# Pairwise merge products in the attention's triangular inverse, an earlier decode of float64 weights, and the experts' low weight parts on another engine

## The chip, the cores and the metric

One core of a Trainium2 chip runs the whole program. The metric is the device time of one execution in microseconds (us); a kernel's time is the median of its runs. A profiled execution of the same program gives the trace from which all rows below come. Engines are named as in the profile: PE (TensorE), PEld (its weight loads), DVE (VectorE), ACT (ScalarE), POOL (GpSimd), SP (SyncE, which here issues nearly all DMAs; SPq is its queue).

## The reference, cut to what matters

Three layers follow one another: a recurrent attention over 768 steps, a routed mixture of eight experts (one expert for each token), and a dense layer with a leaky activation. The matrices `w_in` and `w_out` of the last layer arrive as float64.

```python
# attention: B, H, S, D = 4, 8, 768, 40, all float32
for t in range(S):
    y[:, :, t] = np.einsum('bhd,bhde->bhe', rt, state)
    Sa = np.einsum('bhde,bhe->bhd', state, at)
    state_decay = state * wt[:, :, None, :] - np.einsum('bhd,bhe->bhde', Sa, bt)
    state = state_decay + np.einsum('bhd,bhe->bhde', vt, kt)
x = attn_out.transpose(0, 2, 1, 3).reshape(B * S, H * D)        # 3072 x 320
# experts: w1 (8, 320, 1024), w2 (8, 1024, 320), float32
logits = x @ w_gate; expert_idx = np.argmax(logits, axis=1)
for e in range(8):
    xe = x[expert_idx == e]
    out[expert_idx == e] = gate_w * (np.maximum(xe @ w1[e], 0) @ w2[e])
# last layer: w_in (320, 2048), w_out (2048, 320)
h = out @ w_in
y = (np.maximum(h, 0) + alpha * np.minimum(h, 0)) @ w_out
```

## The kernel before, in words

**Attention** (class `Attention`). The 768 steps are cut into chunks of 64. Four chunks of two batches (16 heads) are a group; there are six groups. Inside a chunk the recurrence becomes products with T, the inverse of a unit triangular 64x64 matrix per head and chunk. `inverse` finds T in two steps. On DVE a loop of 31 steps inverts all 32x32 diagonal blocks at once (`tmp`, `ut`). Then `diagonal` copies the blocks into the tiles `tt`, one tile for each half of a group, and two rounds of small products on PE fill the off-diagonal 32x32 block: `zp` = l1 times the high diagonal block, a copy to `z` on ACT, `yp` = t11 times z, and a copy with a minus sign into `tt` on ACT. A `tt` tile holds for each of two chunks (c2) and eight head pairs (u) a 128x128 block with two heads (q) on its diagonal. These rounds are called merges here: 6 groups x 2 halves x 2 products = 24 products, of 32 matmuls each before the change. `tt` is a ring of three tiles. The main loop has 48 slots; the plan in `run` lays the preparation of the next groups between them. `Router.tiles` turns finished outputs into token rows `xr` and scatters them to `xs_d` in DRAM by GpSimd's indirect DMA.

**Experts** (class `Moe`). For expert e the rows of `xs_d` are loaded (`xe`), transposed and split into a high and a low part; the hidden layer is made in eight blocks f of 128 columns. For each f PE makes `ph` (two PSUM buffers, so PE can be one block ahead), ACT makes `hh` = relu(ph), DVE makes what is missing of it (`hh` for the last 64 columns, and the low part `hl`), and PE then adds the block to the sums `po`. The first expert does its first 256 tokens on their own (`ehh`, `ehl`) and the other 192 after them, in the same eight blocks. At the end `ye` is taken from the sums and written to DRAM.

Beside this, `prep_expert(e + 1, ...)` loads the next expert's weights in six pieces into a ring of three `raw` tiles, ACT makes their high parts and one engine subtracts these from `raw` to give the low parts (`we`, L1058, L1060, L1073). And `decode` turns the 20 pieces of the float64 matrices into float32: DMA of 512 KB into `r64` (two buffers), three integer operations on DVE (`dec`, L214, L215, L216 in `f64_bits`), a range test on ACT (`sq`), DMA back to DRAM.

**The order of the work.** Only the first group's start is written out by hand for DVE, POOL and ACT. All else is placed by a scheduler at build time, which fixes one order for each engine and for SP's queue; at run time each engine goes through its list and waits where an operand is missing. The last layer (`run` from L1237 on) works on 6 blocks of 512 tokens and is the same in both kernels.

Of the kernel before, what the change touches and what calls it, by code (L numbers as in the profile page):

```python
# [8 lines left out]
F32 = mybir.dt.float32  # L9
# [10 lines left out]
P = 128  # L20
# [268 lines left out]
class Attention:  # L289
# [9 lines left out]
    def __init__(self, tc, ctx, k, wP, kbP, aP, rvP, vrow, rt):  # L299
# [34 lines left out]
        self.d1s = ring("d1s", 1, [PP, nw], V, (every, 1e-10), (lambda t: t.rearrange("p (c t) -> p c t", t=CW)[:, :, C:], 1.0), dt=BF16, pool=self.pa)[0]  # L334
        self.d1q = ring("d1q", 1, [PP, nw], V, (every, 0.0), pool=self.pa)[0]
# [21 lines left out]
    def fill(self, out, n):  # L357

        flat = out.rearrange("p c u t -> p (c u t)")
        for _ in range(n):  # L360
            mm(self.nc, flat[:, :P], self.k.ones, self.k.ones, True, True)
# [163 lines left out]
    def inverse(self, o):  # L525
# [8 lines left out]
        for j in range(31):  # L534
            n, m = 31 - j, j + 1
            if o.start:
                tmp = self.pa.tile([P, 256], F32, name="tmp", bufs=1)
                col = ul[:, j, j + 1:]
            else:
                if j == 0:  # L540
                    bank = self.work("tmp", [P, 512], "mg")
                    tmp = bank[:, :256]
                if j in (0, 8, 16):
                    j0, j1 = j, (8, 16, 32)[j // 8]
                    part = bank[:, 256:256 + (j1 - j0) * (32 - j0)].rearrange("p (a b) -> p a b", b=32 - j0)
# [14 lines left out]

        ttc = self.t4("ttc")
# [6 lines left out]
        lows = [slice(q * 64, q * 64 + 32) for q in range(2)]  # L568
        highs = [slice(q * 64 + 32, q * 64 + 64) for q in range(2)]
        both = [(c2, u, q) for c2 in range(2) for u in range(8) for q in range(2)]  # L570
        for half in range(2):
            if half:
                diagonal(1)
# [4 lines left out]
            zp = self.work("zp", [P, 2, 8, 32], "mg" if o.start or half == 0 else "w1")  # L578
            if o.start:
                self.fill(zp, 8)  # L580
            for c2, u, q in both:
                nc.tensor.matmul(zp[lows[q], c2, u], lhsT=l1[highs[q], 2 * half + c2, u, :], rhs=tt[highs[q], c2, u, highs[q]], start=True, stop=True)
            z = self.pa.tile([P, 2, 8, 32], F32, name="z1", tag="z1", bufs=1)
            for lo in lows:
                nc.scalar.copy(z[lo], zp[lo])
            yp = self.work("yp", [P, 2, 8, 32], "mg" if o.start or half == 0 else "w1")
            if o.start:
                self.fill(yp, 8)
            for c2, u, q in both:
                nc.tensor.matmul(yp[lows[q], c2, u], lhsT=t11[lows[q], 2 * half + c2, u, :], rhs=z[lows[q], c2, u, :], start=True, stop=True)  # L590
            for lo, hi in zip(lows, highs):
                nc.scalar.activation(tt[lo, :, :, hi], yp[lo], AF.Copy, scale=-1.0)
# [286 lines left out]
class Router:  # L879
# [39 lines left out]
    def tiles(self, sp, work, b0, t, yt):  # L919

        nc, k = self.nc, self.k
        xr = [sp.tile([P, DM], F32, name="xr", bufs=3) for _ in range(2)]
# [74 lines left out]
class Moe:  # L997
# [142 lines left out]
    def run(self, ctx, to_flag):  # L1140
# [16 lines left out]
        for e in range(E):  # L1157
# [27 lines left out]
            def between(f):  # L1185
# [16 lines left out]
                if (e, f) == (1, 0):  # L1202
# [160 lines left out]
```

## Time and profile before

| | |
|---|---|
| median of 3 runs | 1097.79 us (1097.37 to 1098.29) |
| the profiled execution's own time | 1104.12 us |
| its span, first to last instruction | 1102.4 us |
| PE busy | 995.8 us, 90% of the span |
| DVE busy | 668.2 us, 61% |
| POOL busy | 578.0 us, 52% |
| ACT busy | 531.7 us, 48% |
| mean granted clock of PE | 0.953 |

Busy shares are means over three stages with different limits: attention to about 485 us, experts to about 742 us, the last layer to the end. What a wait costs is read from the stage in which it lies. Matmuls are pipelined, so a row's duration is longer than the step from one matmul to the next.

### The profile page before, as it was taken

To read this page: it belongs to the slowest core of one execution; us is meant where nothing else is said; L and a number is where in the kernel's file an instruction comes from. 1 tells how busy PE (TensorE), PEld (TensorE's weight loads), DVE (VectorE), ACT (ScalarE), POOL (GpSimd) and SP (SyncE) were. 2 spreads that over 40 slices of the span, in tenths; PEclk is the share of its full clock that TensorE was granted. 3 is DMA by queue.
4 is the path that set the end of the run, shared out by engine and by line. 5 is a ranking of instruction groups with operands and counts; after the bars stand their busy time and mean duration, and the time that the engine had idled before them with its cause. 6 is when DMAs were issued, how large, how long until landed. Compare 5 with 4: busy or idle time off the path is not lost.

```text
span 1102.4 us, 25835 instructions
## 1 busy us (share of the span) xinstructions
PE 995.8 (90%) x9981; PEld 883.5 (80%) x9981; DVE 668.2 (61%) x1451; ACT 531.7 (48%) x1255; POOL 578.0 (52%) x592
## 2 busy tenths in 40 slices
PE   3669998889899898889799999999999999999997
PEld 3557777778788777678788889999898898988986
DVE  8895959969688594553679763234444444444532
ACT  3656766677677676644666644431222222221211
POOL 7865665796867544325465544643534343534332
PEclk9669989999899898889999999999999999999999
DMA  4452423333333134417889854420000000000000
GB/s 123 113 188 74 95 66 82 95 87 79 85 84 76 45 71 101 104 37 239 263 278 304 282 162 126 140 70 11 24 25 25 24 25 24 25 24 25 25 1 27
DMA packets 128326, 103.43 MB, mean 94 GB/s; under 512 B 90564, under 2 KB 111044, under 8 KB 128196
## 3 DMA queue, kind: packets, MB, share of 16 engines
q1 hardware_dynamic: 125892, 93.83, 29.8%
q0 software_dynamic: 2304, 7.87, 2.2%
q8 instruction: 81, 1.33, 0.5%
q14 instruction: 49, 0.40, 0.1%
HBM read 79.39 MB, written 22.28 MB: 92 GB/s over the span
## 4 chain that ended last, share of the span: by engine, by line
PE 62%; DVE 21%; DMA 6%; issue 4%; ACT 4%; POOL 3%; SPq 0%; DVEq 0%; POOLq 0%; ACTq 0%
PE ph L243 22%; PE po L243 21%; PE lp L493 3%; PE pp L631 2%; DVE tmp L549 2%; DVE ut L551 2%; DVE s L464 2%; DVE dec L215 2%; DMA raw<-in_moe_w_dram 2%; PE sa L671 2%; PE yc L687 2%; PE rvp L642 2%; DVE va L676 1%; PE ap L517 1%; DVE q L466 1%
## 5 line engine op out<-in xcount | busy, mean ns | idle before, releaser
L234 POOL TENSOR_TENSOR gl<-g,gh 128x512 fp32r<-128x512 f32 x96 | 123.6, 1290 | 214.8 <-ACT gh L233 123.3
L233 ACT ACTIVATE gh<-g 128x512 fp32r<-128x512 f32 x96 | 60.8, 633 | 251.9 <-DVE g L1250 173.2
L1249 DVE TENSOR_SCALAR g<-ph,al 128x512 f32<-128x512 f32 x96 | 72.1, 751 | 160.1 <-POOL gl L234 79.8
L243 PE MATMUL ph<-x2thi,win 128*128 128x512 f32 x480 | 159.5, 397 | 0.0
L243 PE MATMUL po<-wout,gh 128*128 128x320 f32 x768 | 139.0, 310 | 0.0
L243 PEld LDWEIGHTS po<-wout,gh 128*128 128x128 f32 x768 | 122.0, 188 | 5.6
L243 PE MATMUL ph<-x2tlo,win 128*128 128x512 f32 x288 | 114.3, 397 | 0.0
L243 PE MATMUL po<-we,hh 128*128 128x320 f32 x480 | 90.5, 316 | 11.8 <-DVE hh L1122 8.8
L243 PEld LDWEIGHTS ph<-x2thi,win 128*128 128x128 f32 x480 | 88.6, 188 | 14.9
L243 PE MATMUL ph<-xthi,we 128*128 128x448 f32 (+2 forms) x360 | 96.9, 341 | 0.8 <-ACT xthi L273 0.8
L243 PEld LDWEIGHTS po<-we,hh 128*128 128x128 f32 x480 | 73.9, 182 | 16.8 <-DVE hh L1122 10.3
L243 PE MATMUL po<-wout,gl 128*128 128x320 f32 x384 | 82.9, 312 | 0.0
L473 POOL TENSOR_TENSOR abd<-ra,q 40x512 f32<-40x512 f32 x44 | 63.5, 1443 | 25.5 <-PE ap L517 14.0
L493 PE MATMUL lp<-kb,abd 128*128 128x128 f32 x352 | 63.4, 329 | 14.5 <-POOL abd L473 9.6
L243 PE MATMUL ph<-xtlo,we 128*128 128x448 f32 (+2 forms) x216 | 73.4, 341 | 0.3 <-DVE xtlo L276 0.3
L243 PEld LDWEIGHTS ph<-xthi,we 128*128 128x128 f32 x360 | 65.7, 193 | 4.2 <-ACT xthi L273 0.9
L493 PEld LDWEIGHTS lp<-kb,abd 128*128 128x128 f32 x352 | 53.8, 230 | 18.8 <-POOL abd L473 10.2
L1250 DVE SCALAR_TENSOR_TENSOR g<-ph,g 128x512 f32<-128x512 f32 x96 | 66.3, 691 | 3.1
L243 PEld LDWEIGHTS po<-wout,gl 128*128 128x128 f32 x384 | 64.0, 188 | 3.0
L655 POOL TENSOR_SCALAR vg<-sm 40x160 f32<-40x160 f32 x96 | 33.6, 350 | 61.3 <-DVE sm L692 47.7
L551 DVE TENSOR_TENSOR ut<-ut,tmp 128x31 f32<-128x31 f32 (+15 forms) x186 | 62.6, 336 | 3.6
L1058 POOL TENSOR_TENSOR we<-raw,we 128x1024 fp32r<-128x1024 f32 x14 | 34.0, 2441 | 57.3 <-ACT we L1056 56.1
(218 smaller groups left out, 2323.0 us busy)
## 6 DMA issues: line engine op xcount, KB each, us to landing
raw<-in_moe_w_dram SPq DMA_DIRECT2D x16, 512.0 KB
raw<-in_moe_w_dram SPq DMA_DIRECT2D x16, 480.0 KB
kb<-in_kbP_dram SPq DMA_DIRECT2D x44, 160.0 KB
r<-in_moe_w_in_dram SPq DMA_DIRECT2D x10, 512.0 KB
r<-in_moe_w_out_dram SPq DMA_DIRECT2D x10, 512.0 KB
xs_d<-tt SPq DMA_DIRECT2D x8, 560.0 KB
raw<-in_moe_w_dram SPq DMA_DIRECT2D x16, 256.0 KB
wz<-in_wP_dram SPq DMA_DIRECT2D x48, 81.4 KB
```

What stands on the lines that cost most here:

```text
L215: nc.vector.scalar_tensor_tensor(t, up, 0xC0000000, t, op0=ALU.bitwise_and, op1=ALU.bitwise_or)
L233: nc.scalar.activation(hi, src, AF.Copy)
L234: return lo_eng.tensor_tensor(lo, src, f32(hi), op=ALU.subtract)
L243: return nc.tensor.matmul(out, lhsT=lhsT, rhs=rhs, start=start, stop=stop)
L464: nc.vector.tensor_tensor_scan(s[:, ::-1], wz[:, 1:][:, ::-1], self.d1s[:, ::-1], 0.0, ALU.mult, ALU.max)
L473: nc.gpsimd.tensor_tensor(abd[r, :, q * C:(q + 1) * C], ra[r], qc[r, :, :C], op=ALU.mult)
L493: nc.tensor.matmul(lp[:, i], lhsT=abd[:, i, c2, :], rhs=kb[:, i, c2, :], start=True, stop=True)
L551: nc.vector.tensor_tensor(ut[:, j + 1:, :m], ut[:, j + 1:, :m], tv, op=ALU.subtract)
L655: nc.gpsimd.tensor_scalar(self.by2(x.vg[C:PP, :, q, :D]), self.halves(self.sm[q * HQ:q * HQ + D, x.p2]), 1.0, 0.0, op0=ALU.mult, op1=ALU.add)
L1058: eng.tensor_tensor(wt[:, 3 + c, cs], raw, f32(wt[:, c, cs]), op=ALU.subtract)
L1249: nc.vector.tensor_scalar(g, ph, 0.0, al[:, f:f + 1], op0=ALU.min, op1=ALU.mult)
L1250: nc.vector.scalar_tensor_tensor(g, ph, 0.0, g, op0=ALU.max, op1=ALU.add)
```

## The change

Four edits. **Merges:** a product takes both heads of a pair at once: 16 matmuls with 128 contraction rows, 64 columns of weights (the wanted 32 and 32 more whose results are not read) and 64 moving columns. For that the rows of the other head and of the low block must be zero, so `vacant` clears the blocks of `tt` on POOL ahead of each half (not for the first group, whose tiles are cleared as a whole), `z` is one fixed tile that is cleared once at the start, and the copies out of PSUM are four of 256 columns instead of two of 512. **Room:** the first group's `tmp` comes from the ring `t4`, and `xr` has two buffers instead of three. **Low parts:** the experts 1 to 7 get the low parts of their weights from DVE instead of POOL; those of `win` and `wout` stay on POOL. **Decode:** it is called at the first block of expert 0's second part instead of the first block of expert 1.

```diff
+        self.z = ring("z", 1, [P, 2, 8, C], G, (every, 0.0), pool=self.pa)[0]
...
-                tmp = self.pa.tile([P, 256], F32, name="tmp", bufs=1)
+                if j == 0:
+                    tmp = self.pa.tile([P, 1024], F32, name="tmp", tag="t4", bufs=3)
...
+        def vacant(half):
+            if not o.start:
+                for lo, hi in zip(lows, highs):
+                    nc.gpsimd.memset(o.tt[half][lo, :, :, hi], 0.0)
...
+        pairs = [(c2, u) for u in range(8) for c2 in range(2)]
+        out = lambda t, c2, q: t[c2 * 64:c2 * 64 + 32, :, q * 32:q * 32 + 32]
+        heads = lambda t: t.rearrange("p (q s) -> p q s", q=2)
+        wide = lambda t, c, u: t.rearrange("p c u j -> p (c u j)")[:, 32 * (8 * c + u):min(32 * (8 * c + u) + C, 1024)]
...
-            for c2, u, q in both:
-                nc.tensor.matmul(zp[lows[q], c2, u], lhsT=l1[highs[q], 2 * half + c2, u, :], rhs=tt[highs[q], c2, u, highs[q]], start=True, stop=True)
-            z = self.pa.tile([P, 2, 8, 32], F32, name="z1", tag="z1", bufs=1)
-            for lo in lows:
-                nc.scalar.copy(z[lo], zp[lo])
+            for c2, u in pairs:
+                w = wide(l1, 2 * half + c2, u)
+                high = heads(tt[:, c2, u])[:, :, 32:]
+                nc.tensor.matmul(heads(zp[c2 * 64:c2 * 64 + w.shape[1], u]), lhsT=w, rhs=high, start=True, stop=True)
+            z = self.z
+            for c2 in range(2):
+                for q, lo in enumerate(lows):
+                    nc.scalar.copy(z[lo, c2, :, q * 32:q * 32 + 32], out(zp, c2, q))
...
+            for c2, u in pairs:
+                w = wide(t11, 2 * half + c2, u)
+                nc.tensor.matmul(yp[c2 * 64:c2 * 64 + w.shape[1], u], lhsT=w, rhs=z[:, c2, u, :], start=True, stop=True)
+            for c2 in range(2):
+                for q, (lo, hi) in enumerate(zip(lows, highs)):
+                    nc.scalar.activation(tt[lo, c2, :, hi], out(yp, c2, q), AF.Copy, scale=-1.0)
...
-        xr = [sp.tile([P, DM], F32, name="xr", bufs=3) for _ in range(2)]
+        xr = [sp.tile([P, DM], F32, name="xr", bufs=2) for _ in range(2)]
...
-                        whole(self.prep_expert(e + 1, nc.gpsimd))
+                        whole(self.prep_expert(e + 1, nc.vector))
...
-                if (e, f) == (1, 0):
+                if (e, f) == (0, 0):
```

**DVE, second part of expert 0.** Before, the list of DVE from the first of its eight blocks (L1122 makes `hh` and `hl`, L274 the low part of transposed tokens):

```order
L1122 SCALAR_TENSOR_TENSOR hh<-ph,hh 128x64
L1122 SCALAR_TENSOR_TENSOR hl<-ph,hh 128x128
L1122 SCALAR_TENSOR_TENSOR hh<-ph,hh 128x64
L1122 SCALAR_TENSOR_TENSOR hl<-ph,hh 128x128
L1122 SCALAR_TENSOR_TENSOR hh<-ph,hh 128x64
L1122 SCALAR_TENSOR_TENSOR hl<-ph,hh 128x128
L1122 SCALAR_TENSOR_TENSOR hh<-ph,hh 128x64
L1122 SCALAR_TENSOR_TENSOR hl<-ph,hh 128x128
L274 TENSOR_TENSOR xtlo<-tr_ps,xthi 128x448 x2
```

With the change, DVE's list from the second of these blocks to the third (the lines of the new kernel are 18 higher from L1058 on: L1140 is `hh` and `hl`, L1091 the low parts of the second matrix of the next expert):

```order
L1140 SCALAR_TENSOR_TENSOR hh<-ph,hh 128x64
L1140 SCALAR_TENSOR_TENSOR hl<-ph,hh 128x128
L215 SCALAR_TENSOR_TENSOR dec<-r_7150,dec 128x512
L274 TENSOR_TENSOR xtlo<-tr_ps,xthi 128x448
L215 SCALAR_TENSOR_TENSOR dec<-r_7160,dec 128x512
L274 TENSOR_TENSOR xtlo<-tr_ps,xthi 128x448
L216 SCALAR_TENSOR_TENSOR dec<-r_7150,dec 128x512
L1091 TENSOR_TENSOR we_7370<-raw,we_7370 128x960
L216 SCALAR_TENSOR_TENSOR dec<-r_7160,dec 128x512
L1091 TENSOR_TENSOR we_7370<-raw,we_7370 128x960
L1140 SCALAR_TENSOR_TENSOR hh<-ph,hh 128x64
L1140 SCALAR_TENSOR_TENSOR hl<-ph,hh 128x128
```

Between two blocks there stand now pieces of the decode and low parts that wait for their DMA. Counted by the output row L1181 (L1199 now) that ends an expert, DVE's list held 0, 6, 6, 5 and 3 pieces of the decode in experts 0 to 4, and holds 5, 5, 5, 5 and 0 now.

**DVE, from the first block of expert 1 to its second**, with the change (L1199 ends the expert before):

```order
L1140 SCALAR_TENSOR_TENSOR hl<-ph,hh 128x384
L216 SCALAR_TENSOR_TENSOR dec<-r_7190,dec 128x512
L1091 TENSOR_TENSOR we_7594<-raw,we_7594 128x960
L214 TENSOR_SCALAR dec<-r_7200 128x512
L274 TENSOR_TENSOR xtlo<-tr_ps,xthi 64x448
L276 TENSOR_TENSOR xtlo<-tr_ps,xthi 64x448
L1199 TENSOR_TENSOR ye<-po_6962,ye 64x320
L215 SCALAR_TENSOR_TENSOR dec<-r_7200,dec 128x512
L1140 SCALAR_TENSOR_TENSOR hh<-ph,hh 128x64
```

Before, the low part `we` in it was on POOL.

**SP, the DMAs at the start of the experts.** Before:

```order
L1086 DMA xe<-xs_d 64x320
L1055 DMA raw<-in_moe_w_dram 128x1024 x2
L1055 DMA raw<-in_moe_w_dram 64x1024 x2
L1034 DMA r_7724<-in_moe_w_in_dram 128x1024
L1034 DMA r_7734<-in_moe_w_in_dram 128x1024
L1086 DMA xe<-xs_d 128x3x320
```

With the change, in the same place and on to the first pieces of the expert after next:

```order
L1104 DMA xe<-xs_d 64x320
L1052 DMA r_7150<-in_moe_w_in_dram 128x1024
L1052 DMA r_7160<-in_moe_w_in_dram 128x1024
L1073 DMA raw<-in_moe_w_dram 128x1024 x2
L1073 DMA raw<-in_moe_w_dram 64x1024 x2
L1104 DMA xe<-xs_d 128x3x320
L1104 DMA xe<-xs_d 64x320
L1089 DMA raw<-in_moe_w_dram 128x3x320 x2
L1089 DMA raw<-in_moe_w_dram 128x2x320
L1104 DMA xe<-xs_d 128x3x320
L1104 DMA xe<-xs_d 64x320
L1060 DMA w_in<-dec 128x512
```

The first two pieces of the decode have moved ahead of the weights of expert 1, and the write of the first decoded piece stands ahead of the third piece and of the weights of expert 2.

## Rows read from the trace of the kernel before

**Rows 1.** Windows: PE, PEld, DVE, ACT, POOL busy (instructions), clock, DMA share, GB/s

```profile
100.00:480.00 380.00, 336.36 (x5861) 288.07 (x5855) 283.38 (x797) 259.21 (x723) 236.53 (x333) 0.94 0.33 81
...
530.00:650.00 120.00, 109.53 (x606) 98.53 (x606) 97.86 (x143) 75.67 (x141) 65.08 (x28) 0.97 0.85 277
650.00:710.00 60.00, 60.00 (x358) 56.46 (x357) 19.20 (x51) 26.90 (x45) 27.57 (x12) 1.00 0.41 129
```

**Rows 2.** Timeline of ACT: the row that ends experts 4 and 6

```profile
656.47 0.42 ACT L1180 COPY ye<-po 64x320 f32<-64x320 f32 x1 [0.28 <-PE po L243]
...
709.87 0.42 ACT L1180 COPY ye<-po 64x320 f32<-64x320 f32 x1 [0.79 <-PE po L243]
```

**Rows 3.** Timeline of PE: first `ph` of expert 1

```profile
523.65 0.37 PE L243 MATMUL ph<-xthi,we 128*128 128x448 f32 x1
```

**Rows 4.** Chain of waits: first `ph` of expert 5

```profile
652.95 1.61 PE ph L243 x8
```

**Rows 5.** Chain of waits: a landing in the experts with decode

```profile
570.05 6.31 DMA r<-in_moe_w_in_dram
```

**Rows 6.** Timeline of PE: its longest wait in the experts

```profile
538.62 0.41 PE L243 MATMUL po<-we,hh 128*128 128x320 f32 x1 [4.64 <-DVE hh L1122]
```

**Rows 7.** Timeline of DVE, two pieces of the decode

```profile
544.61 0.69 DVE L215 SCALAR_TENSOR_TENSOR dec<-r,dec 128x512 uint32<-128x512 uint32 x1
...
609.38 2.64 DVE L215 SCALAR_TENSOR_TENSOR dec<-r,dec 128x512 uint32<-128x512 uint32 x1
```

**Rows 8.** Timeline of POOL at the second of them

```profile
609.13 5.03 POOL L1073 TENSOR_TENSOR we<-raw,we 128x960 fp32r<-128x960 f32 x2
```

**Rows 9.** Groups by shape, DVE, decode: count, busy us, mean ns, idle before

```profile
L215 DVE SCALAR_TENSOR_TENSOR dec<-r,dec 128x512 uint32<-128x512 uint32 x20 | 27.3, 1369 | 0.4
L216 DVE SCALAR_TENSOR_TENSOR dec<-r,dec 128x512 uint32<-128x512 uint32 x20 | 25.5, 1276 | 0.3
L214 DVE TENSOR_SCALAR dec<-r 128x512 uint32<-128x512 uint32 x20 | 16.7, 837 | 5.8 <-DMA r<-in_moe_w_out_dram 4.5 <-DMA r<-in_moe_w_in_dram 1.3
```

**Rows 10.** Timeline of DVE: a piece's first operation with no POOL work beside it

```profile
544.16 0.42 DVE L214 TENSOR_SCALAR dec<-r 128x512 uint32<-128x512 uint32 x1
```

**Rows 11.** Timeline of DVE: low parts of expert 0, made during the attention

```profile
437.75 1.22 DVE L1058 TENSOR_TENSOR we<-raw,we 128x1024 fp32r<-128x1024 f32 x1 [4.15 <-ACT we L1056]
...
445.82 1.16 DVE L1073 TENSOR_TENSOR we<-raw,we 128x960 fp32r<-128x960 f32 x1 [0.98 <-ACT we L1072]
```

**Rows 12.** Timeline of DVE: `hh` and `hl` in expert 0's second part, `hl` in expert 1

```profile
510.13 0.23 DVE L1122 SCALAR_TENSOR_TENSOR hh<-ph,hh 128x64 fp32r<-128x64 f32 x1 [0.29 <-ACT hh L1119]
510.27 0.28 DVE L1122 SCALAR_TENSOR_TENSOR hl<-ph,hh 128x128 fp32r<-128x128 f32 x1
...
543.70 0.55 DVE L1122 SCALAR_TENSOR_TENSOR hl<-ph,hh 128x384 fp32r<-128x384 f32 x1
```

**Rows 13.** Groups by shape, DVE: token low parts and output rows, 530 to 650 us

```profile
L274 DVE TENSOR_TENSOR xtlo<-tr_ps,xthi 128x448 fp32r<-128x448 f32 x6 | 3.7, 615 | 0.0
...
L1181 DVE TENSOR_TENSOR ye<-po,ye 64x320 f32<-64x320 f32 x4 | 1.9, 476 | 0.0
```

**Rows 14.** Groups by shape, PE: the merge products, and products of 128x64 by 64

```profile
L642 PE MATMUL rvp<-rd,vv 128*64 128x64 f32 x768 | 36.6, 233 | 3.1 <-DMA va<-in_vrow_dram 2.7 <-DVE lg L931 0.3
...
L582 PE MATMUL zp<-tt,l 32*32 32x32 f32 x768 | 19.3, 202 | 11.9 <-DVE tt L559 6.9 <-POOL tt L559 3.1 <-issue 1.6
...
L590 PE MATMUL yp<-z,t 32*32 32x32 f32 x768 | 17.6, 201 | 0.0
```

**Rows 15.** Groups by shape, ACT: copies out of PSUM of 256 and 512 columns

```profile
L644 ACT COPY vg<-rvp 64x256 f32<-64x256 f32 x96 | 35.2, 367 | 5.1 <-PE rvp L642 4.2
...
L585 ACT COPY z<-zp 32x512 f32<-32x512 f32 x24 | 13.8, 575 | 3.6 <-PE zp L582 3.1
```

**Rows 16.** POOL: a memset of 1024 columns (groups by shape)

```profile
L333 POOL MEMSET abd<- 128x1024 f32 x2 | 1.9, 950 | 0.0
```

**Rows 17.** Timeline of POOL in the first microseconds

```profile
7.75 3.56 POOL L473 TENSOR_TENSOR abd<-ra,q 40x512 f32<-40x512 f32 x2
```

More of the change, by code (lines that the diff above doesn't have):

```diff
@@ L357, in fill @@
     def fill(self, out, n):
-        flat = out.rearrange("p c u t -> p (c u t)")
+        flat = out.rearrange("p u t -> p (u t)")
         for _ in range(n):
@@ L553, in inverse @@
                 yield
+        lows = [slice(q * 64, q * 64 + 32) for q in range(2)]
+        highs = [slice(q * 64 + 32, q * 64 + 64) for q in range(2)]
+        def vacant(half):
+            if not o.start:
+                for lo, hi in zip(lows, highs):
+                    nc.gpsimd.memset(o.tt[half][lo, :, :, hi], 0.0)
         def diagonal(half):
@@ L559, in diagonal @@
                 eng.tensor_scalar(o.tt[half][r, :, :, 32 * q:32 * q + 32], ttc[r, 2 * half:2 * half + 2], 1.0, 0.0, op0=ALU.mult, op1=ALU.add)
+        vacant(0)
         ttc = self.t4("ttc")
@@ L566, in inverse @@
         yield
-        lows = [slice(q * 64, q * 64 + 32) for q in range(2)]
-        highs = [slice(q * 64 + 32, q * 64 + 64) for q in range(2)]
-        both = [(c2, u, q) for c2 in range(2) for u in range(8) for q in range(2)]
+        pairs = [(c2, u) for u in range(8) for c2 in range(2)]
+        out = lambda t, c2, q: t[c2 * 64:c2 * 64 + 32, :, q * 32:q * 32 + 32]
+        heads = lambda t: t.rearrange("p (q s) -> p q s", q=2)
+        wide = lambda t, c, u: t.rearrange("p c u j -> p (c u j)")[:, 32 * (8 * c + u):min(32 * (8 * c + u) + C, 1024)]
         for half in range(2):
             if half:
+                vacant(1)
                 diagonal(1)
@@ L577, in inverse @@
             tt = o.tt[half]
-            zp = self.work("zp", [P, 2, 8, 32], "mg" if o.start or half == 0 else "w1")
+            zp = self.work("zp", [P, 8, C], "mg" if o.start or half == 0 else "w1")
             if o.start:
                 self.fill(zp, 8)
-            for c2, u, q in both:
-                nc.tensor.matmul(zp[lows[q], c2, u], lhsT=l1[highs[q], 2 * half + c2, u, :], rhs=tt[highs[q], c2, u, highs[q]], start=True, stop=True)
-            z = self.pa.tile([P, 2, 8, 32], F32, name="z1", tag="z1", bufs=1)
-            for lo in lows:
-                nc.scalar.copy(z[lo], zp[lo])
-            yp = self.work("yp", [P, 2, 8, 32], "mg" if o.start or half == 0 else "w1")
+            for c2, u in pairs:
[6 more added lines that the diff above has]
+                    nc.scalar.copy(z[lo, c2, :, q * 32:q * 32 + 32], out(zp, c2, q))
+            yp = self.work("yp", [P, 8, C], "mg" if o.start or half == 0 else "w1")
             if o.start:
                 self.fill(yp, 8)
[L589 to L592, printed above, removed]
+            for c2, u in pairs:
[4 more added lines that the diff above has]
+                    nc.scalar.activation(tt[lo, c2, :, hi], out(yp, c2, q), AF.Copy, scale=-1.0)
             yield
```

## The prediction

> **What bounds the kernel now.** Busy shares over the whole span say little here, so I cut the span at the stages and read the windows first [rows 1]. In the attention (100 to 480 us) PE is busy 336 of 380 us, ACT 259, POOL 237: PE is nearest to the limit, none is far from it. From 710 us on the code is the same and PE is busy nearly throughout; nothing of the change reaches it. The stretch that gives something is 530 to 650 us, experts 1 to 4 with the decode of the float64 weights. PE runs 606 rows there in 120 us, 5.05 per us; in the next 60 us, without decode, 358, or 5.97 per us, with no idle time. So experts with decode are slower than experts without it. A clean expert takes (709.87 - 656.47) / 2 = 26.7 us from one end to the next, mean of experts 5 and 6 [rows 2]. For the four with decode I need the end of expert 0. PE's first `ph` of expert 1 starts at 523.65 [rows 3]; in the clean stretch the first `ph` of expert 5 (652.95 [rows 4]) starts 3.5 us before expert 4's end at 656.47, so expert 0 "ends" at 527.15 on that scale. From there to 656.47 are 129.3 us for four experts, against 4 x 26.7 = 106.8: 22.5 us too many. That is the purse.
>
> Who holds it? In the chain of waits through that stretch most pieces between two PE pieces are DVE's decode operations (`dec`), and a few are landings of the decode's DMAs, the longest 6.3 us early on [rows 5]. PE's longest wait there is for `hh` from DVE, 4.64 us [rows 6]: DVE works through its list in order, and two whole pieces of decode stood ahead of it there. And why are they so long? The timeline has the same operation, L215 on the same shape, once with 0.69 and once with 2.64 us [rows 7]. In the second case POOL is making low parts in the same microseconds (one starts at 609.13, two take 5.03 [rows 8]) and DVE's operation ends about when POOL's does. So an integer operation of DVE that starts while POOL subtracts is held until POOL is done. The groups show it at large [rows 9]: the 60 operations take 27.3 + 25.5 + 16.7 = 69.5 us. Alone a piece takes 0.42 [rows 10] + 0.69 + 0.69 (L216 as L215, the same number of operands and columns) = 1.80 us, 20 pieces 36 us. POOL's neighbourhood costs DVE 33.5 us.
>
> **The low parts.** They leave POOL, so the 33.5 us go away. DVE gets them instead. Expert 0's were made on DVE already: 1.22 us for 1024 columns and 1.16 for 960 [rows 11], the 640 columns in proportion about 0.8. An expert has three of the first kind (one on half the partitions, taken as equal), two of the second, one of the third: 3.66 + 2.32 + 0.8 = 6.8 us. For experts 1 to 7 that is 47 us, so DVE's total grows by about 14 us, but in pieces of at most 1.2 us instead of 2.7. The cover for it is PE: is DVE's list for one expert shorter than 26.7 us? `hh` and `hl` of one block take 0.14 + 0.55 = 0.69 (the step between the pair, and `hl`'s duration [rows 12]), eight times 5.5; four to six token low parts of 0.62, about 2.5; two output rows of 0.48, about 1.0 [rows 13]; five pieces of decode 9.0; low parts 6.8. Sum 24.8 us: it fits, at 93%, with nothing to spare for landings or for an uneven order. The excerpt of DVE's list in expert 1 shows the unevenness: between two blocks stand 0.69 + 1.16 + 0.42 + 2 x 0.62 + 0.48 + 0.69 = 4.7 us, with the pair 5.4, while PE has 3.23 us of work for a block (652.95's 1.61 for `ph`, as much again for `po`). That is 2.1 us late, and a second place near the expert's end is about as bad. PE is one `ph` ahead, which takes some of it. Bounds for an expert with decode: 26.7 (all covered) and 129.3 / 4 = 32.3 (as now). I take 26.7 + 2.7 = 29.4: two places of 2.1, less PE's slack, and a landing now and then.
>
> **The decode an expert earlier.** This has a price in expert 0. Its second part has only 192 tokens, so its eight blocks are short: 13.5 us from the first `hh` at 510.13 [rows 12] to expert 1's first `ph` at 523.65 [rows 3]. Into this DVE's list now puts four and a half pieces of decode (8.3 us), three low parts of expert 1 (3.1) and three of expert 2 (3.7), beside six token low parts (3.7) and the eight short pairs (0.14 + 0.28 each, together 3.4): 22.2 us instead of 13.5. PE cannot run ahead of it by more than a block. So this part becomes 8.7 us longer by DVE's sum alone. What stands in the list also waits for DMA: SP now issues 1 MB of decode input ahead of expert 1's weights, and the third piece and expert 2's weights are issued only after the first decoded piece is written. Bounds for the jam: 6 us (some of the list slips into expert 1's own time) and 21 (8.7 and two landings like the 6.3 us one on the chain). The `raw` buffers come free sooner than before, though, since a low part takes 1.2 us and not 2.5; I take 9. In return expert 4 has no decode left (by the counts in the change section) and costs about 27.0, with its low parts alone on DVE.
>
> Sum for the experts: 527.15 + 9 + 3 x 29.4 + 27.0 = 651.4 instead of 656.47: 5.1 us gained. The clock comes back by itself in this: it is 0.97 on average in 530 to 650 [rows 1], and PE's pauses only change place. The scatter's third buffer `xr` hides behind four slots of other work between two users, and `tmp` in the ring follows readers long done; if the covers fail, each costs a wait of about one DMA, under 3 us. Both at nothing.
>
> **The merges.** 768 rows of `zp` and 768 of `yp` took 19.3 + 17.6 = 36.9 us [rows 14]. In their place stand 768 rows of 128x64 weights by 64 columns. The trace has exactly 768 rows of that shape, `rvp`: 36.6 us [rows 14]. So on PE the edit is worth nothing, 0.3 us. ACT gets four copies of 256 columns for two of 512: 4 x 0.367 - 2 x 0.575 = +0.32 us for each of 24 products [rows 15], 7.6 us on an engine that is 68% busy there [rows 1]. Exposed it costs 7.6, hidden nothing; the idle column of the old products shows only waits for `tt`, and those on the copies are too small to be named there [rows 14], so I take 0.5. POOL clears two blocks of 512 columns for ten halves: by half of the 0.95 us for 1024 columns [rows 16] about 10 us. They stand a slot ahead of the copies of the diagonal, on tiles long free; POOL has 38% idle. I take nothing; the upper bound is these 10 us. The clearing of `z` does stand on the path: POOL goes without pause into the first `abd` at 7.75 [rows 17], which the first products wait for, and the 0.95 us go in front of it. Together 0.3 less than nothing on PE, +0.5 and +0.95: about 1.2 us lost.
>
> A rule weighs against this edit. The row, once more: 1536 small rows and 768 wide ones of the same total columns take the same time [rows 14]. The Trainium skill, page "TensorEngine Tiling (Array Packing)", section "Theoretical Speedup", says that a product with few contraction rows and few columns can share the array with others, up to 4x and more, so the 32x32 products would be the form to keep. By the rule the wide ones could take twice as long or worse, and the sum would be some 37 us on PE instead of nothing.
>
> **The sum.** -5.1 + 1.2 = -3.9 us on the span. The profiled execution took 1104.12 us around a span of 1102.4, 6.3 over the median of the runs; the difference is carried over: 1097.8 - 3.9 = 1093.9.
>
> **The rivals.** *Full relief*: the jam is 6, experts with decode take 27.4 and the next 26.7, as DVE's sum of 24.8 allows. Then expert 4 ends at 527.15 + 6 + 82.2 + 26.7 = 642.05, 14.4 earlier: 1084.6. For it: nothing is longer than 1.2 us in DVE's list any more. Against it: 93% in a fixed order. *The transfers set the pace*: DMA moves 277 GB/s at 85% busy in this stretch [rows 1], and a piece needs a landing of several us with only two buffers; then experts with decode stay at 31, little under the present 32.3, expert 4 ends at 527.15 + 9 + 93 + 27.0 = 656.15, 0.3 earlier, and with the merges' 1.2 the time is 1098.7. Against it: the 20 pieces need 5 landings per expert, and two buffers overlap them. *A deeper jam*, the other side: a low part now waits for its DMA in DVE's list and holds `hh` behind it, which on POOL it did not. If the jam exceeds 9 + 3.9 = 12.9 us, the change is slower; with one landing and a half on top of 8.7, 18 us, it is 1102.9. Against it: ACT makes the high part from the same landing, just before, and it had `hh` behind it already. *Merges that lose overlap*: the small rows are listed with 202 ns but follow each other every 25 (19.3 / 768), so several are in flight. If wide ones in this place go at twice their time, PE gets up to 37 us more, of which its idle 44 us of 380 hide perhaps half: about 1112. `rvp` speaks against it.
>
> **How the numbers follow.** The forecast has 0.44, with a range of its own of 1090 to 1098; full relief 0.17, the pace of transfers 0.17, the deeper jam 0.13, the merges 0.05; 0.04 stay for an attention whose new order differs by more than its edits. A measurement here can tell 0.2%, 2.2 us. Faster (under 1095.6): 0.31 of the forecast, all full relief, 0.04 of the rest: 0.52. Same: 0.11 of the forecast, 0.12 of the transfers, 0.02 of the jam: 0.25. Slower (over 1100.0): what is left, 0.23, mostly the jam and the merges. For eight times in ten the range goes from 1085, at the edge of full relief, to 1102.5, before the deep jam.
>
> **What would show it.** Right: L215 near 0.7 us throughout; low parts on DVE at 1.2; PE rows per us in the experts 1 to 3 at about 5.4; expert 0 about 9 us longer, expert 4 ending near 652 on the same scale; the merges' rows 37 us in all. Wrong: waits of DVE for landings of several us each in expert 0, experts 1 to 3 still above 31 us, or PE idle at new places in the attention.

## The result and the profile after

The changed kernel takes 1089.02 us (median of four runs, 1085.61 to 1090.49) against 1098.04: ratio 0.9887, interval 0.9851 to 0.9923. A second measurement gave 1084.53 against 1097.23: 0.9872 (0.9833 to 0.991). The forecast was 1093.9 in 1085 to 1102.5. The direction holds; the gain is 9.0 us in the first measurement and 12.7 in the second, 2.3 and 3.3 times the forecast's 3.9, and the second time lies just under the range. The profiled execution took 1090.49 us around a span of 1088.8.

Windows of the changed kernel, the three of [rows 1] and the one between them (columns: PE, PEld, DVE, ACT and POOL busy with instructions, granted clock of PE, DMA share, GB/s):

```profile
100.00:480.00 380.00, 329.66 (x5301) 280.25 (x5300) 291.98 (x813) 267.17 (x774) 246.19 (x352) 0.98 0.34 82
480.00:530.00 50.00, 42.20 (x259) 38.38 (x258) 33.51 (x79) 27.21 (x57) 1.96 (x2) 0.86 0.72 237
530.00:650.00 120.00, 119.71 (x704) 111.61 (x703) 93.91 (x173) 77.40 (x140) 0.00 (x0) 1.00 0.82 264
650.00:710.00 60.00, 57.31 (x356) 54.72 (x355) 18.83 (x48) 25.54 (x46) 26.59 (x13) 0.98 0.39 119
```

PE runs 704 rows in 530 to 650, 5.87 per us, nearly the clean 5.97; POOL does nothing there. The window now takes in expert 4 without decode; in experts 1 to 3 alone it is 489 rows in 82.4 us (their windows stand further down), 5.93 per us, where the prediction expected about 5.4. The attention has changed too, which the forecast did not expect: a granted clock of 0.98 instead of 0.94. Decode and low parts on DVE, against [rows 9]:

```profile
L1091 DVE TENSOR_TENSOR we<-raw,we 128x960 fp32r<-128x960 f32 (+1 forms) x21 | 21.7, 1040 | 4.3 <-ACT we L1090 4.2
L1076 DVE TENSOR_TENSOR we<-raw,we 128x1024 fp32r<-128x1024 f32 x14 | 16.9, 1220 | 3.9 <-ACT we L1074 3.9
L216 DVE SCALAR_TENSOR_TENSOR dec<-r,dec 128x512 uint32<-128x512 uint32 x20 | 13.7, 686 | 0.2
L215 DVE SCALAR_TENSOR_TENSOR dec<-r,dec 128x512 uint32<-128x512 uint32 x20 | 13.7, 686 | 0.3
L214 DVE TENSOR_SCALAR dec<-r 128x512 uint32<-128x512 uint32 x20 | 8.3, 421 | 7.8 <-DMA r<-in_moe_w_in_dram 4.5 <-DMA r<-in_moe_w_out_dram 3.2
```

The three operations take 35.7 us instead of 69.5. The mean of 1040 ns mixes two shapes: 14 low parts of 960 columns at 1152 ns and 7 of 640 at 814. For a comparison of all kernels I cut the traces at ACT's copies `ye`: the first copy of 128 rows ends the first part of expert 0, the copies of 64 rows end the experts. In the changed kernel (start, duration):

```profile
497.41 0.41 ACT L1201 COPY ye<-po 128x320 f32<-128x320 f32 x1
...
529.59 0.42 ACT L1198 COPY ye<-po 64x320 f32<-64x320 f32 x1
...
612.03 0.42 ACT L1198 COPY ye<-po 64x320 f32<-64x320 f32 x1 [0.28 <-PE po L243]
639.97 0.42 ACT L1198 COPY ye<-po 64x320 f32<-64x320 f32 x1 [0.28 <-PE po L243]
```

The steps between these rows are one line of the table: 32.2 us for expert 0's second part, 82.4 for experts 1 to 3, 27.9 for expert 4. "Scatter" is the start of the last pair of POOL's indirect DMAs, "clock" that of 240 to 480 us, "pieces" the decode pieces that begin in experts 0 to 4, all from each run's own trace.

| kernel | ratio | clock | scatter | first `ye` | e0, 2nd part | e1 to e3 | e4 | pieces |
|---|---|---|---|---|---|---|---|---|
| before | 1 | 0.92 | 493.7 | 508.6 | 21.2 | 96.2 | 30.4 | 0 6 6 6 2 |
| changed | 0.989 | 0.98 | 483.0 | 497.4 | 32.2 | 82.4 | 27.9 | 5 5 5 5 0 |
| changed, again | 0.987 | 0.98 | 478.9 | 492.9 | 32.4 | 82.1 | 27.9 | 5 5 5 5 0 |
| merges only | 0.994 | 0.99 | 478.2 | 492.6 | 21.7 | 99.0 | 29.7 | 0 6 6 6 2 |
| fill | 1.004 | 0.96 | 483.5 | 500.2 | 22.1 | 99.3 | 32.3 | 0 6 6 6 2 |
| experts only | 0.992 | 0.91 | 488.2 | 502.9 | 28.2 | 85.2 | 27.9 | 5 5 5 5 0 |
| low parts only | 0.996 | 0.91 | 489.5 | 504.9 | 21.1 | 94.0 | 28.0 | 0 6 7 6 1 |
| decode only | 0.993 | 0.93 | 486.8 | 501.0 | 23.3 | 91.2 | 29.0 | 4 6 5 5 0 |
| late decode | 0.990 | 0.99 | 478.4 | 494.7 | 24.1 | 92.2 | 28.0 | 0 6 7 6 1 |
| late, small loads | 0.994 | 0.97 | 484.4 | 501.1 | 22.6 | 95.4 | 27.9 | 0 7 8 5 0 |
| expert 1 on POOL | 0.983 | 0.96 | 479.1 | 495.4 | 26.4 | 83.0 | 27.5 | 4 6 4 6 0 |
| experts 1, 2 on POOL | 0.985 | 0.98 | 482.9 | 497.1 | 23.3 | 84.0 | 27.5 | 4 6 4 6 0 |

The profile of before is of an execution 6.3 us over its median. Three other traces with the attention as before have the first `ye` at 501.0 to 504.9, not 508.6, so the profiled gain of 11.2 us there is probably too large; 9 us (mean 502.9 against 493.9 in four traces with the new merges, all seven from one chip) is the better value. Every number of this table but the ratio is from one trace of its kernel.

### The profile page after: what moved, and what is told of

Its sections match the earlier page's. It is cut to its first block, busy times and chain, and to the rows that moved or that the text cites. A ratio compares the mean times of both kernels' runs of the same rounds, so it can differ in the third digit from the quotient of the medians.

```text
span 1088.8 us, 24353 instructions
## 1 busy us (share of the span) xinstructions
PE 980.7 (90%) x9213; PEld 871.9 (80%) x9213; DVE 681.9 (63%) x1493; ACT 536.5 (49%) x1303; POOL 490.9 (45%) x571
## 5 line engine op out<-in xcount | busy, mean ns | idle before, releaser
L243 PE MATMUL po<-we,hh 128*128 128x320 f32 (+1 forms) x480 | 92.5, 322 | 6.8 <-ACT hh L1137 6.1
L1076 POOL TENSOR_TENSOR win<-raw,win 128x1024 fp32r<-128x1024 f32 x4 | 9.6, 2406 | 185.3 <-ACT win L1074 185.2
L243 PEld LDWEIGHTS po<-we,hh 128*128 128x128 f32 (+1 forms) x480 | 75.9, 187 | 10.7 <-ACT hh L1137 6.7
L494 PE MATMUL lp<-kb,abd 128*128 128x128 f32 x352 | 58.2, 309 | 17.2 <-POOL abd L474 10.3
L494 PEld LDWEIGHTS lp<-kb,abd 128*128 128x128 f32 x352 | 49.1, 212 | 21.6 <-POOL abd L474 10.8
L689 PE MATMUL sa<-vg,pw 128*64 128x104 f32 x768 | 57.2, 262 | 6.8 <-issue 4.6
```

The lines of the kernel that those rows point to most:

```text
L243: return nc.tensor.matmul(out, lhsT=lhsT, rhs=rhs, start=start, stop=stop)
L494: nc.tensor.matmul(lp[:, i], lhsT=abd[:, i, c2, :], rhs=kb[:, i, c2, :], start=True, stop=True)
L689: nc.tensor.matmul(sa[q * 64:q * 64 + 64, i], lhsT=x.pw[:, i, q * C:(q + 1) * C], rhs=x.vg[:, i, q, :], start=True, stop=True)
L1076: eng.tensor_tensor(wt[:, 3 + c, cs], raw, f32(wt[:, c, cs]), op=ALU.subtract)
```

## The experiments

**The merges alone**, the changed kernel with both edits of the experts taken back:

```diff
-                        whole(self.prep_expert(e + 1, nc.vector))
+                        whole(self.prep_expert(e + 1, nc.gpsimd))
...
-                if (e, f) == (0, 0):
+                if (e, f) == (1, 0):
```

> The attention's edits alone (wide products for zp and yp, halves cleared on GpSimd, four copies, the fixed z, tmp in the ring, two xr buffers); experts as before. Theory of the prediction: nothing on PE, 0.95 us for the clearing of z and 0.5 us of copies, so +1.2 us, which no measurement here tells from 0; the last scatter of the attention ends within 2 us of the kernel before in the trace. Rival: the 10 us by which the attention of the changed kernel ended earlier in its trace are the edits' own; then this kernel is 5 to 11 us faster, its last scatter ends near 483 instead of 494, and the experts behind it take as long as before. Third case: the 10 us belong to one profiled execution (its granted clock fell to 0.74 and 0.84 in two windows of 20 us); then ratio 1.00 within 0.2% while the traces differ by their clocks alone.

Measured: 0.9939 (0.991 to 0.9968), 5.0 us in the medians, with the last scatter at 478.2. The rival holds in the main and the +1.2 us fell: the attention's early end is the edits' own. The experts behind it are not as before, though: with the same operations in the same order on every engine, experts 0 to 4 take 150.4 us instead of 147.9, and expert 7 takes 2.2 more. So about half of the gain is lost again. The price of the rows does not explain the early end, as these groups of the changed kernel show beside [rows 14]:

```profile
L660 PE MATMUL rvp<-rd,vv 128*64 128x64 f32 x768 | 36.0, 232 | 1.2 <-DVE lg L949 1.0
L607 PE MATMUL yp<-z,t 128*64 128x64 f32 x372 | 16.1, 232 | 3.3 <-ACT z L601 3.3
L597 PE MATMUL zp<-tt,l 128*64 128x64 f32 x372 | 15.5, 233 | 10.6 <-DVE tt L569 7.3 <-POOL tt L569 3.3
L607 PE MATMUL yp<-z,t 128*32 128x64 f32 x12 | 1.9, 246 | 0.0
L597 PE MATMUL zp<-tt,l 128*32 128x64 f32 x12 | 1.8, 232 | 0.0
```

Together 35.3 us against 36.9, 1.6 less. But cut finely, the windows around the last group's merges differ in the clock. First the kernel with the experts' edits alone (attention as before), whose small products lie at 412 to 428 us, then the changed kernel, whose wide ones lie at 415 to 425:

```profile
410.00:420.00 10.00, 8.39 (x242) 7.18 (x240) 6.86 (x18) 6.39 (x14) 7.53 (x13) 0.73 0.27 56
420.00:430.00 10.00, 9.93 (x144) 8.84 (x146) 0.84 (x2) 5.68 (x14) 2.86 (x6) 0.50 0.25 74
430.00:440.00 10.00, 6.55 (x82) 5.66 (x80) 4.86 (x7) 5.48 (x9) 1.80 (x4) 0.84 0.96 243
440.00:450.00 10.00, 9.54 (x130) 7.64 (x129) 6.34 (x15) 6.77 (x16) 2.56 (x4) 0.73 0.29 73
```
```profile
410.00:420.00 10.00, 8.66 (x204) 7.83 (x204) 8.45 (x23) 7.25 (x19) 7.41 (x15) 1.00 0.30 62
420.00:430.00 10.00, 8.82 (x171) 7.40 (x169) 1.26 (x4) 9.25 (x24) 5.19 (x8) 1.00 0.48 148
430.00:440.00 10.00, 8.22 (x128) 6.86 (x123) 5.81 (x14) 6.16 (x14) 1.99 (x4) 1.00 0.78 165
440.00:450.00 10.00, 7.93 (x101) 6.84 (x103) 6.84 (x12) 7.49 (x17) 2.76 (x4) 0.66 0.47 117
```

With the small products the clock falls inside the first window and is 0.50 in the next, the lower of its two levels (1.2 GHz), with PE busy 9.93 of 10 us; with the wide ones it stays at 2.4 GHz until 440. In time: DVE's last `ttc`, the transpose just ahead of these merges, starts at 409.1 to 410.9 us in the three traces with small products from one chip and at 409.3 to 409.9 in the four with wide ones from the same chip: the two forms stand level there. From it to the scatter are 75.9 to 79.3 us in all four traces with small products, at a mean granted clock of 0.78 to 0.87, and 68.6 to 73.5 us in all seven with wide ones, at 0.91 to 0.98. So the whole gain lies behind the last merges, and it goes with the clock. The fall is not at the same place in every trace: with small products and the early decode alone, the clock is 1.00 from 420 to 430 and falls later, to 0.71 from 440 to 450, and that is the stretch of 75.9 us.

**Fill.** To separate the clock from copies, clearing and room, the kernel before got four products of 128x128 ahead of each group of merge products (the first group had eight already), nothing else:

```diff
-            if o.start:
-                self.fill(zp, 8)
+            self.fill(zp, 8 if o.start else 4)     # the same ahead of yp
```

> The kernel before with four extra products of 128x128 ones into each merge's PSUM tile ahead of the 32x32 products (results not read; 5 groups x 4 products x 4 = 80 more matmuls, about 4 us of PE at the full clock); nothing else is changed. Clock theory (the attention gains because the clock falls to its lower level right after the 32x32 merges and not after the wide ones): the granted clock between 240 and 480 us rises from 0.91 to 0.93 to 0.96 or more, the last scatter comes some 4 to 6 us earlier than in the runs with the attention as before (486.8 to 493.7), and the kernel is 2 to 5 us faster in spite of the added work. Rival (the copies, the clearing or the free PE queue give the gain): the clock stays at 0.91 to 0.93, and the kernel is the same or up to 5 us slower. Third: four products are too few to hold the clock; then clock and time stay as in the rival, and only the clock rows tell it.

The same windows:

```profile
410.00:420.00 10.00, 8.53 (x205) 6.96 (x199) 9.56 (x27) 6.84 (x17) 5.97 (x11) 1.00 0.24 51
420.00:430.00 10.00, 9.84 (x302) 8.51 (x294) 3.20 (x9) 8.49 (x21) 6.80 (x12) 1.00 0.34 80
430.00:440.00 10.00, 8.69 (x161) 7.77 (x155) 5.03 (x15) 7.15 (x15) 1.98 (x4) 1.00 0.87 229
440.00:450.00 10.00, 7.37 (x121) 5.79 (x118) 8.55 (x15) 8.28 (x18) 3.18 (x5) 1.00 0.62 160
```

Small products, old copies, and yet 1.00 throughout. From the last `ttc` (413.4) to the scatter are 70.1 us at a mean clock of 0.98, as with wide products. For this stretch the clock is thus shown to be what the gain hangs on. The kernel's time does not confirm it: it is slower, 1.0038 (1.001 to 1.0065), where 2 to 5 us faster were expected. Its last `ttc` comes about 3 us later than in the three traces with small products from the same chip, and from the scatter to the first `ye` it takes 16.7 us instead of 14.2 to 15.4, so the first `ye` comes only 2.7 us before the 502.9 of the attention as before. Then experts 0 to 4 take 153.6 us instead of 147.9. That is not another plan: from 480 us on, through all experts, both traces show the same operations, by tile and shape, in the same order on each of PE, DVE, ACT, POOL and SP. Of the 5.7 us PE is idle for 2.8 and busy for 3.0, with the granted clock at 0.95 instead of 0.98 over experts 0 to 4. What made these waits and this clock is open.

**The experts' edits alone**, attention as before:

```diff
-                        whole(self.prep_expert(e + 1, nc.gpsimd))
+                        whole(self.prep_expert(e + 1, nc.vector))
-                if (e, f) == (1, 0):
+                if (e, f) == (0, 0):
```

> The experts' edits alone (low parts on DVE, decode from expert 0 on); attention as before. Theory of the prediction: the jam in expert 0's second part costs 9 us and experts 1 to 4 give back 14 to 17, so 5 to 8 us faster, less some 3 us that the tail gives back if that belongs to the experts' new order. Rival: the gain is the attention's; then this one is within 2 us of the kernel before. With the run of the attention's edits alone the two gains should add up to that of the whole change, 9 to 12 us; if they don't, the parts act on each other.

Measured: 0.9919 (0.9888 to 0.995). Experts 0 to 4 take 141.2 us, 6.7 less. Its 8 per mille and the 6 of the merges make 14, against 11 and 13 for the whole: the parts add up within their intervals. Expert 2 takes 31.7 us here, with five pieces of the decode, its neighbours 27.0 and 26.5.

**Each half of the experts' edits**, first the low parts on DVE (first pair of the diff above), then the early decode (second pair):

> The low parts of the weights on DVE alone; decode still from expert 1 on, attention as before. Theory (an integer operation on DVE is held while GpSimd subtracts): the three decode operations fall to 0.42, 0.69 and 0.69 us, no jam in expert 0 beyond some 3 us for the three low parts of expert 1, experts 1 to 4 take 27.3 to 28.5 us each instead of 32.3, expert 4 ends 13 to 17 us earlier and the kernel is 10 to 17 us faster. Rival (transfers pace the decode): the operations are as short, but experts 1 to 4 stay above 31 us and the gain is under 4 us.

> The decode from expert 0 on alone; low parts on GpSimd as before, attention as before. Theory (what helps is GpSimd leaving, the early start only moves the work): the decode operations stay at a mean of 0.84 to 1.37 us, expert 0's second part takes 9 to 16 us longer than its 13.5, expert 4 is free of decode and gives back about 5; the result is 0 to 10 us slower. Rival (the early start spreads the decode and is what helps): 3 us or more faster.

Both theories missed, and both results lie where the rivals put them. The low parts alone give 0.9959 (0.9928 to 0.9991), 3.5 us in the medians where 10 to 17 were expected and under 4 by the rival; experts 1 to 3 stay at 31.3 us on the mean. The early decode alone gives 0.9928 (0.9897 to 0.9958), faster by 6.6 us where 0 to 10 us slower were expected. Low parts only, on DVE:

```profile
L215 DVE SCALAR_TENSOR_TENSOR dec<-r,dec 128x512 uint32<-128x512 uint32 x20 | 13.8, 690 | 0.3
L216 DVE SCALAR_TENSOR_TENSOR dec<-r,dec 128x512 uint32<-128x512 uint32 x20 | 13.7, 687 | 0.3
L214 DVE TENSOR_SCALAR dec<-r 128x512 uint32<-128x512 uint32 x20 | 8.4, 422 | 13.1 <-DMA r<-in_moe_w_out_dram 8.6 <-DMA r<-in_moe_w_in_dram 4.4
```

The hold by POOL is gone, as forecast: 35.9 us. The Trainium skill, page "SBUF — State Buffer", section "SBUF: two separate sides", describes this as an exclusive lock on a port pair that DVE and GpSimd share; the rows agree, 69.5 us with POOL's subtractions beside DVE's operations and 35.9 without. Yet experts 1 to 3 go from 96.2 only to 94.0. DVE now has 47 us of low parts instead and waits 13.1 us for landings; that these two hold the experts up is argued, not shown. With the decode early and POOL still at work, DVE's holds remain (timeline of the decode-only kernel, expert 0's second part):

```profile
502.04 4.92 DVE L214 TENSOR_SCALAR dec<-r 128x512 uint32<-128x512 uint32 x2
506.87 0.21 DVE L1122 SCALAR_TENSOR_TENSOR hh<-ph,hh 128x64 fp32r<-128x64 f32 x1
...
507.20 2.98 DVE L215 SCALAR_TENSOR_TENSOR dec<-r,dec 128x512 uint32<-128x512 uint32 x2
```

Two L214 take 4.92 us there, but this part grows by only 2.1 us, and experts 1 to 4 take 6.4 less than before.

**The late decode**, all of the change but the early start:

```diff
-                if (e, f) == (0, 0):
+                if (e, f) == (1, 0):
```

> The change without its early decode (decode called at expert 1's first block, as before; all else as changed). Theory from the runs of single parts: with the low parts on VectorE experts 1 to 3 take about 31 us instead of 28, since decode and weights share the transfers in fewer microseconds, and expert 0 loses its jam of 9 to 10 us: end of expert 4 the same within 3 us, result 0 to 5 us slower than the changed kernel. Rival of the prediction (VectorE's list is the bound, full relief): experts at 28 us without the jam, 7 to 10 us faster than the changed kernel.

Measured: 0.9901 (0.9865 to 0.9938), 2.1 us over the changed kernel in the medians, as expected but inside the intervals. Windows from end to end of experts 1, 2 and 3, first with the late decode, then of the changed kernel:

```profile
518.79:550.02 31.23, 28.61 (x164) 25.49 (x163) 25.42 (x49) 20.22 (x40) 0.00 (x0) 1.00 0.94 299
550.02:580.68 30.66, 28.87 (x166) 26.43 (x167) 25.13 (x48) 20.59 (x40) 0.00 (x0) 1.00 0.88 295
580.68:611.01 30.33, 28.42 (x162) 25.20 (x162) 25.10 (x48) 20.54 (x42) 0.00 (x0) 1.00 0.89 293
```
```profile
529.59:556.22 26.63, 26.63 (x159) 25.10 (x158) 23.79 (x44) 20.14 (x37) 0.00 (x0) 1.00 1.00 330
556.22:583.53 27.31, 27.31 (x164) 25.75 (x163) 23.90 (x46) 19.06 (x36) 0.00 (x0) 1.00 0.96 317
583.53:612.03 28.50, 28.21 (x166) 26.00 (x165) 23.41 (x46) 19.11 (x36) 0.00 (x0) 1.00 0.85 276
```

With five pieces per expert PE has no idle time in experts 1 and 2, at a DMA share of 1.00 and 0.96. With 6, 7 and 6 it stands idle for about 2 us in each, and its rows are busy for up to 2 us longer. Between the two kernels experts 1 to 3 differ by 9.8 us and expert 0's second part by 8.1 the other way; five pieces of 1.80 us are 9.0. Beside the new merges and with the low parts on DVE, the early start hardly gains: it moves five pieces from one place to another.

**Late decode with small loads.** The DMA share of 0.88 to 0.94 made the transfers a suspect. This kernel leaves out seven eighths of 18 of the 20 loads, so its decoded matrices are not the reference's (beside the late decode):

```diff
-            r64 = self.r6.tile([P, n, 2], U32, name="r64", bufs=2)
-            nc.sync.dma_start(r64, wo[:, c:c + n])
...
+            r64 = self.r64[self.n_small % 2]
+            m = n if self.n_small < 2 else 64
+            nc.sync.dma_start(r64[:, :m], wo[:, c:c + m])
```

> The run with the late decode (all of the change but the early decode), with 18 of the 20 loads of float64 words cut to an eighth of their columns (two fixed buffers, loaded in full by the first two pieces; every operation and every wait stays; of the output, the decoded matrices are wrong, so the last layer works on other numbers). Question: what holds experts 1 to 3 at 30 to 31 us there. Transfers theory: VectorE waited 11.4 us there for landings of these words, and DMA was 88 to 94% busy; with an eighth of the bytes experts 1 to 3 take 28 us or less on the mean and the kernel is 6 to 9 us faster than with the late decode, 1078 to 1081. Rival (VectorE's list of 6 to 8 pieces per expert is the bound): experts 1 to 3 stay at 30 us or more, within 2 us of 1086.6.

Measured: 0.9938 (0.9912 to 0.9965), not faster. Expert 2 and what DVE waited for in experts 1 to 3 (sum, times, longest):

```profile
554.92:587.00 32.08, 29.10 (x167) 26.15 (x166) 27.36 (x53) 22.45 (x45) 0.00 (x0) 1.00 0.66 201
```
```profile
DVE dec L214 <- DMA r<-in_moe_w_out_dram: 7.7, 5, 3.4
DVE dec L214 <- DMA r<-in_moe_w_in_dram: 2.6, 2, 1.8
```

The share falls to 0.66 and the expert still takes 32.1 us; the waits for landings stay, 10.3 us against 11.4 with the full loads. The volume of these loads is not the bound; the transfers theory falls in that form. When the loads are issued and land was not varied. But expert 3, with five pieces here, takes 32.1 us too, so a count of pieces alone does not explain it either. Which chain of waits through the fixed lists of DVE and SP it is stays open.

**Low parts of expert 1 back on POOL**, aimed at the jam:

```diff
-                        whole(self.prep_expert(e + 1, nc.vector))
+                        whole(self.prep_expert(e + 1, nc.vector if e else nc.gpsimd))
```

> The changed kernel with the low parts of expert 1's weights alone back on GpSimd (those of experts 2 to 7 stay on VectorE). Theory: VectorE's list in expert 0's second part loses three low parts (3.6 us) and the order puts the pairs of hh closer; the jam falls from 9 to 10 to about 2 to 4 us, as in the run with the early decode alone (23.3 us from the first part's ye to the end, against 32.2), while experts 1 to 4 keep 28 to 29 us each: 4 to 8 us faster than the changed kernel, if the transfers leave that. Rival (transfers set the pace from the first piece on): experts 1 to 3 get longer by what the jam gives, and the result is within 2 us of the changed kernel. Other side: GpSimd's six subtractions hold decode operations and with them hh for 5 us or more, slower.

> The fastest version so far (low parts of expert 1's weights on GpSimd) with those of expert 2 on GpSimd as well; experts 3 to 7 stay on VectorE. Theory: GpSimd's subtractions fall into expert 1, which has six pieces of decode, and each holds an operation for 1 to 2 us; but VectorE's list there loses six low parts (6.8 us). Two effects of like size: within 3 us of that version, expert 1 at 28 to 30 us (28.8 before). Rival: VectorE's list was the bound in expert 1 (28.8 against the clean 26.7); then it falls to 27 and the kernel is 2 to 3 us faster.

With expert 1 on POOL 1079.45 us, 0.983 (0.9798 to 0.9861), the fastest here. Expert 0's second part takes 26.4 us instead of 32.4 (a jam of 5.2, not 2 to 4), experts 1 to 3 83.0 instead of 82.1; the gain is inside the 4 to 8 us expected. On the same chip its six runs lie at 1075.72 to 1081.76, the changed kernel's at 1078.26 to 1088.7: 5.1 us in the medians, though the intervals of the ratios overlap. The hold is there, and cheap at this place:

```profile
496.36 4.34 DVE L214 TENSOR_SCALAR dec<-r 128x512 uint32<-128x512 uint32 x2
500.64 0.20 DVE L1140 SCALAR_TENSOR_TENSOR hh<-ph,hh 128x64 fp32r<-128x64 f32 x1
```

Expert 2 on POOL as well gives nothing more: 0.9851 (0.9813 to 0.989), with expert 1 at 30.3 us, just over the 28 to 30 of the theory. Expert 0's second part takes 23.3 us there at a granted clock of 1.00, against 26.4 at 0.81 with expert 1 alone on POOL (the runs also differ in where expert 2's first low parts are made). And expert 3 takes 27.1 and 27.2 us in these two runs with six pieces of the decode. This run and that with small loads were on another chip, where before took 1102.93.

**The changed kernel again**, unedited:

> The changed kernel once more, for a narrower interval and a second trace. From the runs of the two parts (-6.1 and -8.1 per mille) a sum of -14; by the first runs -11. Expected 0.986 to 0.990. In the trace: clock 0.97 or more between 240 and 480 us, last scatter 478 to 484, expert 0's second part 22 to 24 us from the first hh to expert 1's first ph, experts 1 to 4 at 28 us each. If the early end of the attention belonged to single executions, the last scatter would come near 490 here.

As expected but for experts 1 to 3, 27.4 instead of 28 us each.

## Why the prediction was right, and where it was not

**The low parts.** Right: L215 fell to 0.69 us, the low parts take 1.22 and 1.15, and the holds went away, 35.7 us instead of 69.5. Right too that the low parts come back as DVE's own work: moving them alone is worth 4 per mille.

**The jam.** Right in place; the size was met partly by luck. Forecast 9 us; from the first `hh` at 501.01 to expert 1's first `ph` at 524.20 are 23.2 us instead of 13.5: 9.7. Timeline of DVE in the changed kernel, then of PE:

```profile
498.11 1.23 DVE L1076 TENSOR_TENSOR we<-raw,we 128x1024 fp32r<-128x1024 f32 x1
499.76 1.22 DVE L1078 TENSOR_TENSOR we<-raw,we 64x1024 fp32r<-64x1024 f32 x1 [0.43 <-ACT we L1074]
501.01 0.23 DVE L1140 SCALAR_TENSOR_TENSOR hh<-ph,hh 128x64 fp32r<-128x64 f32 x1
...
508.11 0.21 DVE L1140 SCALAR_TENSOR_TENSOR hh<-ph,hh 128x64 fp32r<-128x64 f32 x1
...
515.21 0.43 DVE L214 TENSOR_SCALAR dec<-r 128x512 uint32<-128x512 uint32 x1 [4.47 <-DMA r<-in_moe_w_in_dram]
```
```profile
511.55 0.72 PE L270 MATMUL tr_ps<-ident,xe 128*128 128x128 f32 x4 [2.99 <-DMA xe<-xs_d]
...
524.20 0.57 PE L243 MATMUL ph<-xthi,we 128*128 128x448 f32 x1
```

DVE's list (low parts, decode, token parts) separates the pairs of `hh`, as forecast, and one landing of 4.47 us holds it; PE waits 2.99 us for token rows `xe` from DRAM. But DVE is busy for 16.9 of these 23.2 us, not for 22.2, so its list alone does not make the length. Expert 0's whole second part, in the changed kernel and then before:

```profile
497.41:529.59 32.18, 25.11 (x129) 22.18 (x130) 25.11 (x50) 20.56 (x43) 0.00 (x0) 0.79 0.80 261
```
```profile
508.60:529.80 21.20, 19.60 (x135) 17.77 (x136) 8.57 (x27) 12.24 (x23) 13.99 (x7) 1.00 0.70 208
```

Of the 11.0 us more, PE is idle for 5.5 and busy for 5.5, with no more rows than before, at a granted clock of 0.79 instead of 1.00. The prediction had put the clock at nothing, since PE's pauses would only change place. Its sum also left out the two low parts ahead of the first `hh`, another 2 us.

**Experts 1 to 3** were mis-sized: 29.4 each with the decode, measured 82.4 / 3 = 27.5, the full relief's 27.4. The two late places of 2.1 us did not appear: PE ran without idle time in experts 1 and 2, with DVE busy for 23.8 of 26.6 and 23.9 of 27.3 us (the sum had 24.8). Expert 4 took 27.9 against 27.0. Over experts 0 to 4 the trace gives 142.6 us instead of 147.9, 5.3 gained where 5.1 were forecast: jam and relief both came out larger, and their errors cancel. That this sum fits is luck, the more so as the experts' lists of before took 147.9, 150.4 (merges only) and 153.6 us (fill) in three traces, so that one trace gives this gain only to within several us. The changed kernel's two traces give 142.6 and 142.4.

**The merges** are the step that failed: +1.2 us, where the attention gains about 9. The parts of the sum that could be read are right: PE's rows 35.3 us, ACT's copies 0.362 and 0.373 us each, 48 of each kind, and half a clear on POOL 0.516 us. Left out was what the products do to the granted clock of the products behind them: a mean of 0.78 to 0.87 from the last `ttc` to the scatter with small ones, 0.91 to 0.98 with wide ones. The profile of before showed 0.94 in the attention [rows 1], and the sum has no term for it. "An attention whose new order differs by more than its edits" had 0.04; it is the edit itself. So the measured time lies in the range, but most of the gain comes from a term that the sum had as a loss.

**The rule against the wide products.** By the prediction's estimate from the Trainium skill, page "TensorEngine Tiling (Array Packing)", section "Theoretical Speedup", they would have been some 37 us dearer. The rows above do not bear it out: 35.3 us against 36.9.

**What is given back.** The prediction said that nothing of the change reaches past 710 us. From expert 5's end to expert 7's the changed kernel takes 60.2 and 60.0 us, merges only 59.6, before 57.4, experts only 57.4, expert 1 on POOL 58.1. So some 2 to 3 us of the gain are lost again in most kernels with the new merges. The loss lies in expert 7: where it takes 34.4 to 35.3 us its granted clock is 0.95, in all other traces it takes 32.0 to 33.0 at 1.00. What lowers the clock there was not tried.

The account: 9 + 5.3 - 2.8 = 11.5 us, against 9.0 in the medians of the first measurement and 12.7 in those of the second.

## What to carry to other kernels

Read the granted clock in short windows around every group of small products, and behind every pause of PE that a change makes, before rows are priced: an edit that is worth nothing in rows was worth 9 us here in what follows it. Where work moves from one engine's list to another's, sum the lists place by place: the short stage pays for what is put into it, and a neighbour's hold cost little in expert 0's second part. Before a difference is put down to the order of the lists, compare the lists: here equal lists took 147.9 to 153.6 us. And take a second trace of before: its profiled attention was about 6 us slower than that of three others with the same code there.

## What the runs showed of the hardware

After 32x32 products the granted clock fell to 0.50 and 0.51 in two of four traces, from 420 to 430 us, while PE was busy 9.93 and 9.81 of 10 us; in the other two it was 0.68 and 1.00 in that window. Four 128x128 products ahead of each group of them kept it at 1.00 from 410 to 450 us, though not at every merge of the run (0.83 on the mean of 360 to 380 us). DVE's decode operations took 69.5 us with POOL's subtractions beside them and 35.9 without. Expert 2 took 27.3 us without PE waiting at a DMA share of 0.96 and 317 GB/s, and 32.1 us in the kernel with small loads at a share of 0.66.
